# Packing the length-47 Fourier steps of a filter and mixer kernel into quarters of the TensorE array

## The chip, the cores and the metric

One core of one Trainium2 chip runs the whole kernel. The metric is the device time of one execution in microseconds. Three executions of the kernel before gave 2565.34, 2567.13 and 2570.79 us; the median, 2567.13 us, is the time before.

## The reference: what is computed

Two blocks follow each other, for a batch of 8 sequences of 3008 rows and 256 channels.

```python
def _attn_ref(x, filt_r, filt_i):            # x: (8, 3008, 256)
    X = np.fft.rfft(x, axis=1)
    F = (filt_r + 1j * filt_i)[None, :, :]   # filter: (1505, 256), real and imaginary part
    y = np.fft.irfft(X * F, n=x.shape[1], axis=1)
    return y.astype(np.float32)

def _moe_ref(x, w_tok1, w_tok2, w_ch1, w_ch2):   # (3008,256) (256,3008) (256,1536) (1536,256)
    xt = x.transpose(0, 2, 1)
    h = np.maximum(xt @ w_tok1, 0.0) @ w_tok2
    u = x + h.transpose(0, 2, 1)
    h2 = np.maximum(u @ w_ch1, 0.0) @ w_ch2
    return (u + h2).astype(np.float32)
```

The first block is a real Fourier transform along the sequence, a product with a complex filter, and the transform back. The second is an MLP mixer: a token MLP along the sequence, and a channel MLP on its sum with the input. All weights of the mixer arrive as 64-bit floats.

## The kernel before, in words

**The transform.** 3008 is 47 x 64. A row number is n2 * 47 + n1, with n2 below 64 and n1 below 47. The transform goes in three steps, forward and back:

- *Length 64* (`a_unit`, L471). One matmul takes two residues n1 = a (partitions 0 to 63) and n1 = a + 24 (partitions 64 to 127), with their 64 values of n2 on the partitions. The table `wa` gives, for each of 32 frequencies k2, four rows: real and imaginary part of either residue. Each matmul carries 2 values of a and 256 channels, so 512 columns. ScalarE copies the bank into `t1`, and a DMA from the ACT queue stores it in `z_d` in device memory, so that the next step can read it with the 96 rows (4 kinds x 24 values of a) of one k2 on the partitions.
- *Length 47* (`b_unit`, L537). For each k2 one matmul of 96 rows by 128 columns makes the real parts (columns 0 to 63) and imaginary parts (64 to 127) of the 47 frequencies that k2 stands for, for both batches of a group side by side (512 columns), or one batch (256).
- *The filter* (L550 to L553): four VectorE operations multiply the bank by the complex filter into `p1`.
- *Length 47 back* (`bi_unit`, L562): one matmul of 128 rows by 96 columns. ScalarE copies the bank into `t3` (L568), and after two frequencies a DMA from the ACT queue stores `t3` in `g_d` (L573).
- *Length 64 back* is no step of its own: `t4_load` (L619) reads `g_d` with the 128 rows of (k2, kind) on the partitions, and the mixer's matmuls take it from there (`token_sums` L625 with the table folded into `w1`, `u_filter` L647 with `wai`).

The batches form the groups (0), (1, 2), (3, 4), (5, 6), (7). Batch 0 keeps its z on the chip (`turned`), takes banks "pg", and multiplies real and imaginary filter at once (L545); its length-47 matmuls are a branch of their own.

**The mixer.** `mix` runs, for each batch and each of 6 row tiles m (512 rows, the last 448), 6 steps jp of 256 hidden channels: 36 items a batch. Its matrix products are done in blocks of two by two with seven products instead of eight, so VectorE adds blocks (helper `v`, L726) before and after them. An item issues, in this order:

1. `up_first` (L748, 4 products of 256 columns), `up_middle` (L726), then the block sums and the first part of `down` (L782, 3 products) of the item before; then place 0.
2. `up_last` (L764, 3 products, two L726 adds, each followed by a ReLU on ScalarE, L769); then place 1.
3. The second part of `down` (L782, 4 products), at a tile's end the first of the steps of `finish`; then place 2.

At certain items and places `u_parts` issues one of the four quarters (`u_quarter`, L669, L675) of the next tile's u, and after the last of them queues two VectorE steps (`v_steps`) and a weight load (`w2m_load`) on SP's queue.

**How the two are interleaved.** The order on every engine is the order in which the program is written (`tc.manual_schedule()`). The transform of the next group is a Python generator, `dft`; at a place that is "due" the loop at the end takes one step from it. For the groups after the first, one step is due at place 1 of each item: a length-64 step, or `b_unit(k)` followed by `bi_unit(k - 1)`. In the items of batch 0 the steps are spread over two places by a counter (L1006 to L1022).

**Banks.** Length-64 and length-47 matmuls, u-quarters and token sums use the two PSUM banks "acc" and "b" in turn:

```python
turn, held = ["acc", "b"], []

def free_bank():
    turn.reverse()
    if turn[0] in held:
        turn.reverse()
    return turn[0]
```

`b_unit` puts its bank into `held`, and `bi_unit` takes it out and writes the products back into the same bank.

**Loads.** `t2_load` (z, from SP's queue) and `w_load` (the length-47 tables `wb` from SP's queue and filter rows) are issued two chunks of two frequencies ahead, with `b_unit` of the even k.

Of the kernel before, what the change touches and what calls it, by code (L numbers as in the profile page):

```python
# [26 lines left out]
KR = 4 * A  # L27
HALF = 64
# [26 lines left out]
def _make_tables():  # L55

    n2 = np.arange(N2)
    wa = np.zeros((P, P))
    wai = np.zeros((P, P))
    for h in range(2):
        r = slice(h * 64, h * 64 + 64)
        for k2 in range(K2):
            th = 2 * np.pi * ((n2 * k2) % N2) / N2  # L70
            c, s = np.cos(th), np.sin(th)
            re, im = 4 * k2 + 2 * h, 4 * k2 + 2 * h + 1
            wa[r, re] = c
            wai[re, r] = c * (1.0 if k2 == 0 else 2.0)
            if k2 == 0:
                alt = 1.0 - 2.0 * (n2 % 2)
                wa[r, im] = alt
                wai[im, r] = alt
            else:
                wa[r, im] = -s  # L80
                wai[im, r] = -2.0 * s
    n1 = np.arange(N1)
    re = (n1 // A) * (2 * A) + n1 % A
    im = re + A
    wb = np.zeros((KR, K2, P))
    wi = np.zeros((P, K2, KR))
    for k2 in range(K2):
        for s in range(2 * A):
# [10 lines left out]
            if edge:  # L99
                sn = np.zeros(N1)  # L100
            if k2:
                wb[re, k2, q] = c
                wb[im, k2, q] = sign * sn
                wb[re, k2, HALF + q] = -sn
                wb[im, k2, HALF + q] = sign * c
            else:
                src = re if s < A else im
                wb[src, k2, q] = c
                wb[src, k2, HALF + q] = -sn
                m = 1.0 if edge else 2.0  # L110
                wi[q, k2, src] = m * c
                wi[HALF + q, k2, src] = -m * sn
    wi[:, 1:, :] = wb[:, 1:, :].transpose(2, 1, 0)
    wi /= N
    f = np.float32
    wbi = np.zeros((P, K2, P + KR))
    wbi[0:KR, :, 0:P] = wb
    wbi[:, :, P:] = wi

    wa0 = wa.reshape(P, K2, 4).transpose(0, 2, 1).reshape(P, P)  # L120
    wbi0 = wbi.copy()
    wbi0[:, :, 0:P] = 0
    wbi0.reshape(4, K2, K2, P + KR)[:, 0:A, :, 0:P] = wb.reshape(4, A, K2, P)
# [4 lines left out]
def kernel(  # L128
# [22 lines left out]

    z_d = nc.dram_tensor("z_tmp", (B, K2, KR, D), FP32, kind="Internal").ap()
    g_d = nc.dram_tensor("g_tmp", (B, K2, KR, D), FP32, kind="Internal").ap()
# [158 lines left out]
    def w1_load(i):  # L312
# [6 lines left out]
        for h in range(2):  # L319
            n = 1 if last and h else 2  # L320
            lo = h * A + 2 * i
            q.dma_start(st[h * HALF:(h + 1) * HALF, 0:n * DT].rearrange("p (a t) -> p a t", t=DT),
                        rows[:, lo:lo + n, :])
# [7 lines left out]
    def w2_load(i):  # L331
# [5 lines left out]
        more = g + 1 < W2G  # L337
        st = stage(512)
        nc.gpsimd.dma_start(st[:, 0:n + more], moe_w_tok2[ts(t, P), ds(g * NG * N1, n + more)])
# [3 lines left out]
        def some(h, nh, w):  # L343
            return (lambda v: bass.AP(tensor=v.tensor, offset=v.offset + h * A, ap=[v.ap[0], [A, nh], [N1, nn], [1, w]]),
                    dst[:, h:h + nh, :, 0:w])

        parts = [some(0, 2, A)] if more else [some(0, 1, A), some(1, 1, A - 1)]
        if i < BY_PE:
            h = halves(st, n + more, spare_pair())
            yield next(h)  # L350
            yield next(h)
            on_chip(ident, *next(h), n + more, parts)
        else:
            yield from rounded(st, n + more, parts, False)
# [90 lines left out]
    def x_load(b, c, i, queue=None):  # L445
# [9 lines left out]
        rows = x[b].rearrange("(n2 n1) d -> n2 n1 d", n1=N1)[:, :, ds(d0 * dc, dc)]  # L455
        for h in range(2):
            n = xc - 1 if h and (c + 1) * xc == A else xc
            lo = h * A + c * xc
            q = queue or (nc.gpsimd if b == 0 and h else nc.sync)
            q.dma_start(t[h * HALF:(h + 1) * HALF, 0:n, :], rows[:, lo:lo + n, :])  # L460
            if n < xc:

                q.dma_start(t[h * HALF:(h + 1) * HALF, n:xc, :], rows[:, lo:lo + 1, :])
        xs[b, c + d0 * (A // xc)] = t

    def rows_of(t_d, b):
        return t_d[b].rearrange("k (g a) d -> (k g) a d", a=A)
# [12 lines left out]
    def dft(bs):  # L480
# [5 lines left out]
        def table_load(c):  # L486
            if c * KC % WC == 0:
                g = c * KC // WC
                where, tag = (t1p, "t1") if first and g % 5 > 2 else (wbp, "wb")
                wbs[g] = where.tile([P, WC, P + KR], FP32, tag=tag, name="wb")  # L490
# [16 lines left out]
        if not first:  # L507
            yield True
        for i, u in enumerate(todo):
# [6 lines left out]
            yield i + 1 < len(todo)  # L516
# [7 lines left out]
        def t2_load(c):  # L524
            if first:
                return
            t2s[c] = t2p.tile([KR, KC, nb, D], FP32, tag="t2", name="t2")
            for i, b in enumerate(bs):
                nc.sync.dma_start(t2s[c][:, :, i, :], z_d[b, ts(c, KC)].rearrange("k r d -> r k d"))

        def b_unit(k):
            tag = "pg" if first else free_bank()
            if not first:
                held.append(tag)
            ps = bank(tag).rearrange("p (b d) -> p b d", b=2)[:, 0:nb, :]
            t2 = turned[:, k, :].unsqueeze(1) if first else t2s[k // KC][:, k % KC]
            nc.tensor.matmul(ps, wbs[k // WC][0:P if first else KR, k % WC, 0:P], t2, start=True, stop=True)  # L537
            re, im = slice(0, HALF), slice(HALF, P)
            t = filts_0[k // KC % len(filts_0)] if first else filts[k // KC % FB]
# [513 lines left out]
```

## Time and profile before

| What | Value |
|---|---|
| Median of three runs | 2567.13 us |
| Span of the profiled execution, first to last instruction | 2563.4 us |
| Median less span (start, end, and the spread of runs) | 3.7 us |
| TensorE matmul busy | 2485.5 us, 11204 instructions |
| VectorE busy | 1919.6 us |
| ScalarE busy | 680.1 us |
| GpSimd busy | 593.2 us |
| Mean granted TensorE clock | 0.994 |
| Moved by DMA | 248.37 MB in 166432 packets |

Busy time of an engine counts a stretch in which several of its instructions overlap once. "PEld" is TensorE's weight load, which runs beside the matmuls. A matmul's own duration includes the time until its last result is out, so the next one can start before it ends; the chain of waits shows how long each held the path. A group's line gives the mean duration of one, then the idle time of the engine just before such an instruction, and what ended that idle time. The page's tenths are busy shares of 40 equal slices of the span.

The length-64 matmuls of the groups lie at 144 to 226 us, 526 to 705 us, 1136 to 1315 us and 1746 to 1832 us of the span, and the length-47 matmuls at 240 to 462 us, 725 to 1023 us, 1335 to 1633 us and 1853 to 2124 us.

### The profile page before, as it was taken

To read this page: it belongs to the slowest core of one execution; us is meant where nothing else is said; L and a number is where in the kernel's file an instruction comes from. 1 tells how busy PE (TensorE), PEld (TensorE's weight loads), DVE (VectorE), ACT (ScalarE), POOL (GpSimd) and SP (SyncE) were. 2 spreads that over 40 slices of the span, in tenths; PEclk is the share of its full clock that TensorE was granted. 3 is DMA by queue.
4 is the path that set the end of the run, shared out by engine and by line. 5 is a ranking of instruction groups with operands and counts; after the bars stand their busy time and mean duration, and the time that the engine had idled before them with its cause. 6 is when DMAs were issued, how large, how long until landed. Compare 5 with 4: busy or idle time off the path is not lost.

```text
span 2563.4 us, 32297 instructions
## 1 busy us (share of the span) xinstructions
PE 2485.5 (97%) x11204; PEld 2049.0 (80%) x11204; DVE 1919.6 (75%) x3594; ACT 680.1 (27%) x1342; POOL 593.2 (23%) x1075
## 2 busy tenths in 40 slices
PE   7889999999999999999999999999999999999997
PEld 4557666888888777888888777898888888898887
DVE  7797888576686988756676899757788587757776
ACT  5633222122221222222222222212222122212222
POOL 6573222112111121121121111211211121211222
PEclk8999999999999999999999999999999999999999
DMA  9974344233332332213333333213333222101100
GB/s 220 248 218 134 118 125 146 70 115 109 116 108 72 107 96 83 81 57 125 101 101 93 97 106 102 85 32 111 103 109 97 58 76 71 44 29 36 43 14 20
DMA packets 166432, 248.37 MB, mean 97 GB/s; under 512 B 35300, under 2 KB 112474, under 8 KB 166270
## 3 DMA queue, kind: packets, MB, share of 16 engines
q1 hardware_dynamic: 93006, 150.24, 19.5%
q0 software_dynamic: 33312, 48.47, 7.5%
q10 hardware_dynamic: 39952, 47.61, 5.9%
q8 instruction: 89, 1.46, 0.2%
q14 instruction: 73, 0.60, 0.1%
HBM read 168.96 MB, written 77.22 MB: 96 GB/s over the span
## 4 chain that ended last, share of the span: by engine, by line
PE 74%; DVE 17%; DMA 4%; issue 2%; ACT 2%; POOL 1%; ACTq 0%; DVEq 0%; SPq 0%; POOLq 0%
PE ps_po L782 25%; PE ps_pg L748 15%; PE ps_pg L764 11%; PE ps_b L625 4%; DVE t L726 3%; DVE hh L726 3%; PE ps_acc L669 2%; PE ps_b L669 2%; PE ps_acc L625 2%; DVE u L726 2%; DVE s L726 2%; DMA filt<-in_filt_r_dram 2%; PE ps_acc L647 2%; PE ps_b L647 2%; PE ps_b L537 1%
## 5 line engine op out<-in xcount | busy, mean ns | idle before, releaser
L827 POOL DMA_DIRECT2D out_dram<-r x757 | 410.5, 551 | 1757.3 <-ACT hh L769 732.7
L726 DVE TENSOR_TENSOR hh<-ps_pg,s 128x512 f32<-128x512 f32 (+3 forms) x864 | 482.7, 586 | 342.2 <-ACT s L751 334.5
L769 ACT ACTIVATE hh<-hh 128x512 f32<-128x512 f32 (+1 forms) x576 | 348.0, 621 | 1200.4 <-DVE hh L726 1200.4
L782 PE MATMUL ps_po<-t,wc 128*128 128x256 f32 (+1 forms) x2304 | 535.7, 375 | 6.7 <-DVE t L726 5.7
L782 PEld LDWEIGHTS ps_po<-t,wc 128*128 128x128 f32 x2304 | 434.1, 190 | 131.8 <-issue 52.9
L748 PE MATMUL ps_pg<-v,wc 128*128 128x256 f32 (+1 forms) x1728 | 413.1, 375 | 3.1 <-DVE v L726 2.4
L782 PE MATMUL ps_po<-hh,wc 128*128 128x256 f32 (+1 forms) x1728 | 412.7, 375 | 0.9 <-POOL wc L363 0.7
L748 PEld LDWEIGHTS ps_pg<-v,wc 128*128 128x128 f32 x1728 | 327.4, 190 | 43.0 <-DVE v L726 5.1
L782 PEld LDWEIGHTS ps_po<-hh,wc 128*128 128x128 f32 x1728 | 327.9, 190 | 38.9 <-POOL wc L363 1.1
L764 PE MATMUL ps_pg<-u,wc 128*128 128x256 f32 (+1 forms) x1152 | 293.5, 377 | 7.2 <-DVE hh L726 7.1
L726 DVE TENSOR_TENSOR t<-t,hh 128x256 f32<-128x256 f32 (+1 forms) x576 | 245.8, 427 | 19.8
L764 PEld LDWEIGHTS ps_pg<-u,wc 128*128 128x128 f32 x1152 | 216.1, 190 | 43.5 <-DVE hh L726 18.4
L726 DVE TENSOR_TENSOR s<-ps_pg,hh 128x512 f32<-128x512 f32 (+1 forms) x288 | 196.0, 681 | 30.4 <-DVE hh L726 0.5
L726 DVE TENSOR_TENSOR t<-hh 128x512 f32<-128x512 f32 (+1 forms) x288 | 193.0, 670 | 0.6 <-ACT hh L769 0.6
L751 ACT COPY s<-ps_pg 128x256 f32<-128x256 f32 (+1 forms) x288 | 105.9, 368 | 312.3 <-PE ps_pg L748 308.5
L748 PE MATMUL ps_pg<-u,wc 128*128 128x256 f32 (+1 forms) x576 | 169.1, 375 | 3.9 <-DVE hh L726 3.9
L764 PE MATMUL ps_pg<-v,wc 128*128 128x256 f32 (+1 forms) x576 | 168.7, 375 | 0.0
L748 PEld LDWEIGHTS ps_pg<-u,wc 128*128 128x128 f32 x576 | 109.0, 190 | 28.9 <-issue 11.0
L764 PEld LDWEIGHTS ps_pg<-v,wc 128*128 128x128 f32 x576 | 108.7, 190 | 13.1
L726 DVE TENSOR_TENSOR u<-ps_acc,u 128x512 f32<-128x512 f32 (+3 forms) x105 | 61.1, 582 | 76.5 <-PE ps_acc L669 60.0
L625 PE MATMUL ps_b<-t,w 128*128 128x256 f32 x480 | 104.6, 379 | 1.1 <-ACT t L568 1.1
L726 DVE TENSOR_TENSOR u<-ps_b,u 128x256 f32<-128x256 f32 (+3 forms) x105 | 59.5, 566 | 61.3 <-PE ps_b L669 42.3
(133 smaller groups left out, 2528.6 us busy)
## 6 DMA issues: line engine op xcount, KB each, us to landing
w<-w_tmp SPq DMA_DIRECT2D x35, 896.0 KB
g_tmp<-t ACTq DMA_DIRECT2D x128, 192.0 KB
out_dram<-r POOLq DMA_DIRECT2D x698, 32.0 KB, 1.8
z_tmp<-t ACTq DMA_DIRECT2D x84, 256.0 KB
t<-z_tmp SPq DMA_DIRECT2D x112, 192.0 KB
t<-g_tmp SPq DMA_DIRECT2D x42, 512.0 KB
wb<-wbi_t SPq DMA_DIRECT2D x80, 224.0 KB
x<-in_x_dram SPq DMA_DIRECT2D x139, 128.0 KB
```

Of the source, the lines that this page charges most:

```text
L537: nc.tensor.matmul(ps, wbs[k // WC][0:P if first else KR, k % WC, 0:P], t2, start=True, stop=True)
L625: nc.tensor.matmul(acc[:, t, :], w1[:, a, ts(t, P)], t4[b, a // TC4][:, a % TC4, :], start=(a == 0 and t == 0), stop=(a == A - 1 and t == ...
L647: nc.tensor.matmul(ps[:, ds(q * P, n)], t4[b, c][:, r, ts(dh, P)], wai[:, 0:n], start=(first and q == 0), stop=(not first and q == 3))
L669: nc.tensor.matmul(ps[:, ds(j * hw, hw)], h1[:, n, :], w2m[m % 2][:, at, 0:hw], start=(i < 2 and j == 0), stop=(j == len(todo) - 1))
L726: nc.vector.tensor_tensor(out=out, in0=in0, in1=in1, op=op)
L748: nc.tensor.matmul(ps[:, 0:hw], chan[0][:, jp, n, :], mov, start=True, stop=True)
L751: nc.scalar.copy(out=s[:, 0], in_=g[0][:, 0, 0:hw])
L764: nc.tensor.matmul(ps[:, 0:hw], chan[0][:, jp, n, :], mov, start=True, stop=True)
L769: nc.scalar.activation(out=hs, in_=hs, func=AF.Relu)
L782: nc.tensor.matmul(po[i][:, j, 0:hw], chan[1][:, jp, n, :], mov, start=(jp == 0 and first == 1), stop=(jp == JP - 1 and last == 1))
L827: q.dma_start(rows[g, e, :, ds(h * A + 4 * m, n)], blocks[ts(g, CW), h, e, 0:n])
```

## The change: what it does

The rows of the input are taken in mirrored pairs. A length-64 matmul now takes residue 23 - a in partitions 0 to 63 and residue 24 + a (shifted by one in n2 where it wraps around) in partitions 64 to 127, so that the two stand at equal distances from the middle. Its table gives, instead of real and imaginary parts of either residue, sums and differences of the pair. With these the length-47 step falls into two independent blocks: 48 of the 96 rows make the real outputs and the other 48 make the imaginary outputs. A block is 48 rows by 64 columns, and backward 64 rows by 64 columns, of which 48 are used.

Two frequencies are then taken together. For odd k2 the two blocks' places are swapped, so that the four blocks of an even and an odd frequency lie in the four 64 x 64 quarters of the array: frequency i and row half h write output half h XOR i of bank i. `b_pair` makes the two frequencies of a chunk in both banks, `multiply` does the four VectorE operations of one frequency, and `bi_pair` goes back, two banks again. A chunk is now three steps of the generator: `b_pair` with the first `multiply` and the loads for two chunks ahead; the second `multiply`; and `bi_pair` with its two ScalarE copies and two stores. For the groups after the first, one chunk takes two items: `b_pair` at place 1 of an odd item, the second `multiply` at place 0 of the next even one, `bi_pair` at place 0 of the next odd one. The u-quarters move to places at which a bank is free.

`z_d` and `g_d` become one tensor for each group, with the group's batches side by side, so that loads of z and stores of g move one 2 KB run for two batches. Because the residues of one half run backward, the loads of x and of `w_tok1`, the rounding of `w_tok2` and the stores of the output go through that half with a negative step. Batch 0 keeps its branch of full matmuls with new tables.

The core of the diff:

```diff
         for h in range(2):
             n = xc - 1 if h and (c + 1) * xc == A else xc
-            lo = h * A + c * xc
             q = queue or (nc.gpsimd if b == 0 and h else nc.sync)
-            q.dma_start(t[h * HALF:(h + 1) * HALF, 0:n, :], rows[:, lo:lo + n, :])
+            q.dma_start(t[h * HALF:(h + 1) * HALF, 0:n, :],
+                        rows(A + c * xc if h else A - 1 - c * xc, [[N1 * D, N2], [D if h else -D, n]]))
...
+        def four(pss, stat, mov):
+            for i, ps in enumerate(pss):
+                for h in range(2):
+                    to = slice((h ^ i) * HALF, (h ^ i) * HALF + HALF)
+                    nc.tensor.matmul(ps[to], stat(i, h), mov(i, h), start=True, stop=True)
+
+        def b_pair(c):
+            prods[c] = two_banks()
+            held.extend(turn)
+            four(prods[c], lambda i, h: wbs[c][ds(h * HALF, KH), i, 0:HALF], lambda i, h: t2s[c][ds(h * HALF, KH), i])
+
+        def multiply(c, i):
+            ps, t = prods[c][i], filts[c % FB]
             re, im = slice(0, HALF), slice(HALF, P)
...
             nc.vector.tensor_tensor(out=p1, in0=ps, in1=fr, op=ALU.mult)
             nc.vector.scalar_tensor_tensor(out=p2[re], in0=ps[im], scalar=-1.0, in1=fi, op0=ALU.mult, op1=ALU.mult)
             nc.vector.tensor_tensor(out=p2[im], in0=ps[re], in1=fi, op=ALU.mult)
             nc.vector.tensor_tensor(out=p1, in0=p1, in1=p2, op=ALU.add)
+            prods[c][i] = p1
+            held.pop(0)
+
+        def bi_pair(c):
+            pss, p = two_banks(), prods.pop(c)
+            four(pss, lambda i, h: wbs[c][ts(h, HALF), i, HALF:P], lambda i, h: p[i][ts(h, HALF)])
+            t3 = t3p.tile([P, KC, nb, D], FP32, tag="t3", name="t3")
+            for i in range(KC):
+                by_block(t3[:, i], pss[i])
+            for h in range(2):
+                nc.scalar.dma_start(g_d[place_of[bs[0]][0]][ts(c, KC), ts(h, KH)].rearrange("k r b d -> r k b d"),
+                                    t3[ds(h * HALF, KH)])
...
+        if not first:
+            for c in range(K2 // KC):
+                b_pair(c)
+                multiply(c, 0)
+                if c + 2 < K2 // KC:
+                    t2_load(c + 2)
+                    w_load(c + 2)
+                yield "m"
+                multiply(c, 1)
+                yield "i"
+                bi_pair(c)
+                if c + 1 < K2 // KC:
+                    yield "b"
+            return
...
-        own = ({(3, 2): 0, (4, 2): 1}, {(2, 2): 0, (3, 0): 1, (3, 2): 2, (4, 0): 3})
-        new = {(JP - 3, 2): 0, (JP - 2, 0): 1, (JP - 2, 2): 2, (JP - 1, 0): 3}
+        own = ({(3, 2): (0,), (4, 2): (1,)}, {(2, 2): (0,), (4, 0): (1,), (4, 2): (2, 3)})
+        new = {(JP - 2, 0): (0,), (JP - 2, 2): (1, 2, 3)}
...
-            due = place == 1
             if group == 0:
-                due = spread
-                if not spread and place:
-                    at += 1
-                    due = at * left // places > (at - 1) * left // places or at > places
+                due = coming in "aw" or place > 0 or (coming == "m" and i % 4 == 2)
+            elif coming in "bmi":
+                due = i % 2 == (coming != "m") and place == (coming == "b")
+            else:
+                due = place == 1
```

`coming` is the kind of the step that is next: a length-64 step ("a"), the wait for the loads ("w"), `b_pair` ("b"), the second `multiply` ("m") or `bi_pair` ("i").

## The prediction

> **What bounds the kernel now.** I read the page first, then the windows view cut by stages, then the chain of waits inside one stage that the change touches, and last the groups with shapes kept apart.
>
> The page:
>
> ```profile
> span 2563.4 us, 32297 instructions
> PE 2485.5 (97%) x11204; PEld 2049.0 (80%) x11204; DVE 1919.6 (75%) x3594; ACT 680.1 (27%) x1342; POOL 593.2 (23%) x1075
> PE   7889999999999999999999999999999999999997
> DMA  9974344233332332213333333213333222101100
> ```
>
> TensorE is busy from the third slice to the end; the DMA engines are full only in the first two slices. The windows view says how much room the other engines have, first where the length-64 matmuls of batches 3 and 4 run (544 to 683), then where their length-47 matmuls run (856 to 1008). Columns are window, length, then the busy time of PE, PEld, DVE, ACT and POOL, the clock, DMA share and GB/s.
>
> ```profile
> 544.30:683.00 138.70, 138.70 (x632) 115.95 (x631) 94.58 (x180) 39.58 (x78) 25.58 (x48) 1.00 0.35 110
> 856.00:1008.00 152.00, 151.09 (x639) 115.95 (x638) 139.27 (x248) 40.16 (x77) 26.00 (x48) 1.00 0.34 98
> ```
>
> In the second window PE has 0.9 us idle of 152, but VectorE has only 12.7 us idle (92% busy; 68% in the first). TensorE is the bound and VectorE stands close behind, just where the change saves or adds matmul time. The chain of waits in that stage, with start, length, engine, tile, line and number of instructions:
>
> ```profile
> 1004.28 1.10 PE ps_b L537 x2
> 1005.38 0.86 PE ps_acc L562 x2
> 1006.24 1.73 PE ps_po L782 x8
> 1007.97 0.89 PE ps_acc L647 x8
> ```
>
> An fp32 product appears as two instructions ("passes"). Eight passes of 256 columns hold the path for 1.73 us, so 0.216 us each; two of 512 columns hold it 0.86 us, 0.43 us a pass. Each pass starts when the one before has streamed. (1.10 includes a restart after a wait.) The groups by form:
>
> ```profile
> L537 PE MATMUL ps_b<-t,wb 96*128 96x512 f32 x96 | 50.2, 604 | 3.7 <-ACT u L658 2.6 <-ACT t L568 0.5 <-DVE u L726 0.2
> L537 PE MATMUL ps_acc<-t,wb 96*128 96x512 f32 x96 | 49.8, 599 | 1.9 <-ACT u L658 1.4 <-DVE u L726 0.2
> L562 PE MATMUL ps_acc<-p,wb 128*96 128x512 f32 x96 | 49.4, 595 | 3.6 <-DVE p L553 3.6
> L562 PE MATMUL ps_b<-p,wb 128*96 128x512 f32 x96 | 49.3, 594 | 2.9 <-DVE p L553 2.9
> L562 PEld LDWEIGHTS ps_acc<-p,wb 128*96 128x96 f32 x160 | 26.0, 165 | 33.1 <-issue 21.8 <-DVE p L553 7.0 <-ACT t L568 1.5
> L553 DVE TENSOR_TENSOR p<-p,p 128x512 f32<-128x512 f32 x96 | 66.5, 693 | 3.3
> ```
>
> A pass lasts 594 to 604 ns but the next starts 430 ns after it: a tail of 0.17 us is normally covered by the next pass. The weight load of 165 ns is covered too. There are 192 passes of 512 columns on L537, so 96 products forward (three groups of two batches, 32 frequencies each), and 96 back on L562.
>
> **What goes.** For three groups 192 products at 0.86 us: 165 us. For the last batch alone 64 products of 256 columns at 0.43 us: 27.5 us. Together 192.6 us of path, 7.5% of the span. Batch 0 has its own branch and keeps its products.
>
> **What comes on TensorE.** Two frequencies are now four products forward and four back, each 48 or 64 rows by 64 columns, with the full 512 (or 256) moving columns. That is eight passes where there were four. The calls come product after product, so the two passes of one product (same tile) stand next to each other: t0 t0 t1 t1 t2 t2 t3 t3. If different tiles may overlap but starts stay in program order, as every start in this trace does, t0's second pass waits 0.43 us for its first; t1's first starts with it; t1's second waits again, and so on: five steps of 0.43 us instead of four. There are 128 such sets (16 pairs, two directions, four groups): 96 at 512 columns, 32 at 256. 96 x 5 x 0.43 + 32 x 5 x 0.216 = 241 us against 192.6: **+48 us**. The bounds: all four tiles together take two steps, 96 us in all, which is -96; no overlap at all takes eight steps, which is +193. No row here has a tiled matmul. I take five because program order is what the rows show.
>
> The Trainium skill, "TensorE: Matmul & The Clock Gate", The mechanism, says matmuls start and end strictly in order, and that tiles of a pack start about 4 ns apart. No tile runs in this trace; its span model, for one instruction per tile, would make a set of single passes about 0.6 us and speaks for the two-step bound, while its order rule with two passes per product gives the five steps.
>
> **Changing shape.** A set always stands between full-array matmuls (after L782 or L764, before L764 or L782), so there are 256 changes between the whole array and quarters. If the tail of 0.17 us must run out at each: 256 x 0.17 = **+43 us**. Bounds: nothing (the trace goes from 96*128 to 128*96 to 128*128 with no gap on the chain) and 0.17 plus an uncovered weight load of 0.19 (190 ns in the L782 rows): +92. No gain is possible, since an exposed tail only adds. I take 0.17, nearest to a plain end-to-start order. The skill's page "TensorEngine Tiling (Array Packing)", Key Properties, says a change of tiling mode drains the array; that speaks against this change and would make the sum +43 where the L537 to L562 rows alone would make it nothing.
>
> **VectorE and the order of steps.** The four products with the filter per frequency stay: 0.68 + 0.69 + 0.68 + 0.69 = 2.75 us. They came once an item, after the two L726 adds that free the pg banks. Now the first set comes in an odd item's place 1 and the second in the next even item's place 0, ahead of those adds. The adds (0.69 us each) hold up the next L748. Over two items VectorE has 15.1 us busy (139.27 in 18.4 items of 8.25 us) of 16.5; if PE grows by 1.54 us per pair (twice 0.43 for the fifth steps, four tails of 0.17), VectorE's 1.4 us of room doubles and the delay hides. Cover gone, it is up to 1.3 us (the two adds) on 48 pairs: 62 us. I take 0; it is the cover that fails in the rival below. The forward set waits for both banks, so for two ACT copies (0.57 us each on L568) after the backward set of the same item; the six L764 passes between (1.29 us) cover all but about 0.1 us. Behind it on PE would stand L782, on VectorE the multiply. The mixer's four u-quarters move from four places to (2,2), (4,0) and (4,2); their 4.7 us per tile of PE work is the same, and the v sums that follow still have item 5 ahead of the next tile. At nothing.
>
> **DMA and the rest.** x halves and z stores go from 2 KB to 1 KB runs, t4 loads from 4 KB to 1 KB, while z loads and g stores go from 1 KB to 2 KB and tables from 224 to 128 KB: some 23,000 pieces more (x 5,400, z stores 6,900, t4 10,400, from the tiles' partitions and counts) against 18,400 fewer, a net near 5,000 of 166,432 packets, and 6 MB fewer of 248 (64 tables, 96 KB each). At a DMA share of 0.34 these stay hidden; loads of z and tables are issued a pair ahead, some 30 us. If not covered, a late z load shows as a PE wait on L537; the chain in this stage had two pieces of 2.18 us on that load. In the first 180 us, where DMA is the bound, only w_tok1's runs halve (768 pieces; 0.195 x 16 x 2563 us / 93006 = 86 ns a packet, over 16 engines 4 us): 0 to +4, taken as 0, since the page has filter loads and not these ones at the head of the chain. w_tok2's rounding writes two halves in place of one: 14 tiles beside those loads, at nothing; SP, POOL and ACT issue as many DMAs as before, but one more per step for the last batch.
>
> **Sum.** +48 + 43 = +91 us on the profiled 2563.4: 2654.5. The median of the runs, 2567.13, lies 3.7 us above that span, which I take for what lies around it: **2658 us**. Own range: tails at nothing to 0.36 us give +48 to +140, so 2615 to 2707.
>
> **Rivals.**
> *All four tiles at once.* If the second pass of a product does not hold back the next tile, a set takes 0.86 us: -96 + 43 = -53 us, 2514. For it: the four products lie in four different quarters of the array, and write disjoint halves of two banks. Against: the start order seen, and VectorE: in the 152 us window there are only 12.7 us to gain, and the second multiply now stands ahead of the adds. If a quarter of the gain goes there: -40, **2527** (2505 to 2555). It decides as soon as a set stays under 1.38 us: four old steps (1.72) less two tails (0.34).
> *The two row halves run as separate streams.* Then three steps a set: -48 + 43 = -5: **2562**.
> *The tiles do not overlap*, so the change does not do what it says: eight steps: +193 + 43 = +236, **2803**. For it: no overlap of streams is in the trace; against: nothing in the code makes the tiles depend on each other.
>
> **Chances.** Five steps 0.46, four at once 0.38, row halves 0.08, serial 0.08. The measurement can tell about 0.2%, 5 us. Faster: nearly all of the second (0.36) and half of the third (0.04): 0.40. Same: 0.05. Slower: 0.55. The range 2515 to 2705 leaves out the serial case and the tips of the two main ones. The likeliest alone: 2615 to 2707.
>
> **What would show it.** In the profile after, passes of 48*64 and 64*64 come eight to a set. Right: within a set starts alternate between pairs a few ns apart and gaps of 0.43 us, a set takes 2.15 us, and before and after it PE idles about 0.17 us. Wrong: starts of all tiles together, a set near 0.9 us, VectorE above 92% in this stage and PE waiting on L726; or no shared starts and sets of 3.4 us. The stage's item grows from 8.25 us to about 9.0 us in my case (half of 1.54 more), and the 544 to 683 stage, which has no tiles, stays at its pace. A PE wait on L537 for a load would be a cost I put at nothing.

## The result, and the profile after

The changed kernel takes 2613.11 us (median of 4 runs, 2607.77 to 2615.97) against 2567.32 us for the kernel before: ratio 1.0177, 95% interval 1.0163 to 1.0192. It is slower by 46 us. The profiled span grew by 49.0 us, from 2563.4 to 2612.4. The page after:

```profile
span 2612.4 us, 33382 instructions
PE 2469.4 (95%) x11716; PEld 1982.0 (76%) x11716; DVE 1919.3 (73%) x3600; ACT 675.4 (26%) x1348; POOL 594.7 (23%) x1077
PE   7889887899999999999999999999999999999997
PEclk8999899999999999999999999999999999999999
```

TensorE is busy 16 us less and yet the span is longer. What is new is one place in the tenths, from the fifth to the eighth slice (261 to 522 us), where TensorE falls from 9 to 8 and 7 tenths; in the fifth the granted clock falls from 9 to 8 tenths.

The first token-sum matmuls of the eight batches cut the span into stages. The differences after less before, in us, are: to batch 0's token sums 0.0; batch 0 +46.7; then +0.4, +0.1, +1.3, +0.5, +0.3, -1.1 and +0.8. So the loss lies in batch 0's items, beside which the transform of batches 1 and 2 runs, and nothing is won elsewhere. The windows view shows both halves of this, first of the kernel before and then of the one after. Columns: window, length, busy time of PE, PEld, DVE, ACT, POOL, then the granted clock, DMA share and GB/s.

```profile
235.00:455.00 220.00, 207.41 (x818) 147.02 (x817) 183.21 (x315) 56.22 (x106) 67.00 (x112) 1.00 0.44 131
880.00:980.00 100.00, 99.39 (x423) 76.45 (x423) 90.10 (x159) 25.59 (x49) 17.33 (x32) 1.00 0.35 98
```

```profile
235.00:455.00 220.00, 179.95 (x761) 112.23 (x762) 151.65 (x262) 44.12 (x84) 49.19 (x84) 0.92 0.38 100
880.00:980.00 100.00, 93.85 (x466) 70.16 (x465) 89.14 (x158) 23.89 (x48) 17.46 (x32) 1.00 0.36 97
```

In the steady stage (second lines) TensorE's busy time falls by 5.5 us in 100, VectorE's stays, and the pace is the same: TensorE waits where it worked. In batch 0's stage every engine does less in the same 220 us, and the mean granted clock is 0.92: no engine is full (TensorE 82% busy), so a chain of waits sets the pace.

A set in the steady stage, from the timeline of TensorE (start, length, line, tile, number of passes):

```profile
909.79 1.03 PE L813 MATMUL ps_po<-hh,wc 128*128 128x256 f32 x4
910.75 0.65 PE L565 MATMUL ps_acc<-p,wb 64*64 64x512 f32 x2
910.76 0.65 PE L565 MATMUL ps_b<-p,wb 64*64 64x512 f32 x2
911.23 0.59 PE L565 MATMUL ps_acc<-p,wb 64*64 64x512 f32 x2
911.24 0.60 PE L565 MATMUL ps_b<-p,wb 64*64 64x512 f32 x2
911.77 1.13 PE L795 MATMUL ps_pg<-u,wc 128*128 128x256 f32 x4
```

The rows with ps_acc and ps_b hold two quarters each. All four first passes start within some 20 ns, all four second passes 0.48 us later, and the next full matmul 0.54 us after that: two steps, not five. The four L813 passes have streamed at 909.79 + 4 x 0.216 = 910.65, so the set starts 0.10 us later; its second step takes 0.11 us more than a pass of 0.43; its first step 0.05; and the four L795 passes take 0.10 us more than the usual 1.03. That is 0.36 us more than two bare steps would cost, which is put down here to going in and out of quarters, and 1.2 us for a set that cost 1.72.

What TensorE waited for between 235 and 502 us (total us, times, longest):

```profile
PE ps_b L565 <- DVE p L582: 13.3, 5, 2.9
PE ps_pg L795 <- DVE hh L757: 11.4, 5, 3.0
PE ps_acc L565 <- DVE p L582: 8.2, 3, 3.1
```

L582 is the last of the four filter operations: the backward set waits for the second multiply of its pair, 21.5 us in all. In the kernel before, the same wait in the same stage (117 to 474.5 us, token sums to token sums) was 6.5 us:

```profile
PE ps_acc L562 <- DVE p L553: 3.6, 4, 1.3
PE ps_b L562 <- DVE p L553: 2.9, 3, 1.1
```

With the waits goes a slower clock. Over its stage of 404.1 us the changed kernel has TensorE busy for 342.4 us at a mean granted clock of 0.95; the kernel that goes one frequency at a time beside batch 0 (below) has it busy for 324.8 of 358.9 us at 1.00, with as many matmuls. Of the 45.2 us between them, 17.6 us are then longer busy time, which fits the clock (404 x 0.05 = 20), and 27.6 us are idle time. This is an estimate from the two windows.

### The profile page after: what moved, and what is told of

Same layout as the page of the kernel before. It is cut to its first block, busy times and chain, and to the rows that moved or that the text cites. A ratio compares the mean times of both kernels' runs of the same rounds, so it can differ in the third digit from the quotient of the medians.

```text
span 2612.4 us, 33382 instructions
## 1 busy us (share of the span) xinstructions
PE 2469.4 (95%) x11716; PEld 1982.0 (76%) x11716; DVE 1919.3 (73%) x3600; ACT 675.4 (26%) x1348; POOL 594.7 (23%) x1077
## 4 chain that ended last, share of the span: by engine, by line
PE 64%; DVE 20%; issue 2%; ACT 2%; DMA 1%; DVEq 0%; ACTq 0%; POOL 0%; SPq 0%; POOLq 0%
PE ps_po L813 22%; PE ps_pg L779 14%; PE ps_pg L795 9%; PE ps_acc L656 6%; DVE t L757 4%; DVE hh L757 3%; PE ps_b L700 3%; DVE p L581 2%; DVE p L580 2%; DVE s L757 2%; DVE u L757 2%; DVE p L579 2%; PE ps_acc L700 2%; PE ps_b L565 2%; PE ps_acc L678 2%
## 5 line engine op out<-in xcount | busy, mean ns | idle before, releaser
L757 DVE TENSOR_TENSOR hh<-ps_pg,s 128x512 f32<-128x512 f32 (+3 forms) x864 | 482.8, 587 | 362.1 <-ACT s L782 347.5
L813 PE MATMUL ps_po<-t,wc 128*128 128x256 f32 (+1 forms) x2304 | 550.4, 382 | 10.0 <-DVE t L757 8.6
L813 PEld LDWEIGHTS ps_po<-t,wc 128*128 128x128 f32 x2304 | 432.0, 192 | 149.5 <-issue 33.9
L779 PE MATMUL ps_pg<-v,wc 128*128 128x256 f32 (+1 forms) x1728 | 416.5, 377 | 0.2
L813 PE MATMUL ps_po<-hh,wc 128*128 128x256 f32 (+1 forms) x1728 | 414.1, 376 | 0.2 <-ACT hh L800 0.2
L779 PEld LDWEIGHTS ps_pg<-v,wc 128*128 128x128 f32 x1728 | 329.1, 191 | 41.4 <-DVE v L757 3.0
L813 PEld LDWEIGHTS ps_po<-hh,wc 128*128 128x128 f32 x1728 | 329.0, 191 | 39.0 <-ACT s L782 0.7
L795 PE MATMUL ps_pg<-u,wc 128*128 128x256 f32 (+1 forms) x1152 | 297.4, 381 | 18.5 <-DVE hh L757 18.0
L795 PEld LDWEIGHTS ps_pg<-u,wc 128*128 128x128 f32 x1152 | 212.9, 190 | 83.6 <-DVE hh L757 34.9
L757 DVE TENSOR_TENSOR t<-t,hh 128x256 f32<-128x256 f32 (+1 forms) x576 | 245.3, 426 | 19.8
L757 DVE TENSOR_TENSOR s<-ps_pg,hh 128x512 f32<-128x512 f32 (+1 forms) x288 | 196.1, 681 | 32.6 <-DVE hh L757 1.8
L779 PE MATMUL ps_pg<-u,wc 128*128 128x256 f32 (+1 forms) x576 | 174.8, 385 | 23.9 <-DVE hh L757 23.8
L757 DVE TENSOR_TENSOR t<-hh 128x512 f32<-128x512 f32 (+1 forms) x288 | 192.7, 669 | 0.6 <-ACT hh L800 0.6
L795 PE MATMUL ps_pg<-v,wc 128*128 128x256 f32 (+1 forms) x576 | 169.4, 376 | 0.0
L779 PEld LDWEIGHTS ps_pg<-u,wc 128*128 128x128 f32 x576 | 105.9, 190 | 62.3 <-DVE hh L757 36.8
L656 PE MATMUL ps_acc<-t,w 128*128 128x256 f32 x672 | 146.5, 379 | 2.5 <-DVE p L581 2.5
L656 PEld LDWEIGHTS ps_acc<-t,w 128*128 128x128 f32 x672 | 127.4, 190 | 20.5 <-DVE p L581 3.5
L757 DVE TENSOR_TENSOR u<-ps_b,u 128x256 f32<-128x256 f32 (+3 forms) x124 | 69.7, 562 | 86.2 <-PE ps_b L700 60.0
L795 PEld LDWEIGHTS ps_pg<-v,wc 128*128 128x128 f32 x576 | 108.9, 190 | 13.4 <-DVE s L757 0.6
```

Source lines behind the costliest of these rows:

```text
L656: nc.tensor.matmul(acc[:, t, :], w1[:, a, ts(t, P)], t4[b, a // TC4][:, a % TC4, :], start=(a == 0 and t == 0), stop=(a == A - 1 and t == ...
L757: nc.vector.tensor_tensor(out=out, in0=in0, in1=in1, op=op)
L779: nc.tensor.matmul(ps[:, 0:hw], chan[0][:, jp, n, :], mov, start=True, stop=True)
L795: nc.tensor.matmul(ps[:, 0:hw], chan[0][:, jp, n, :], mov, start=True, stop=True)
L813: nc.tensor.matmul(po[i][:, j, 0:hw], chan[1][:, jp, n, :], mov, start=(jp == 0 and first == 1), stop=(jp == JP - 1 and last == 1))
```

## The experiments

The measure besides the total is the pace of one row tile beside length-47 sets: the difference between the starts of the first L779 (before: L748) matmul of row tiles 1 and 2 of batch 2. It is 52.39 us before and 52.95 us after. "Batch 0's stage" is the time from batch 0's first token-sum matmul to batch 1's: 357.4 us before, 404.1 after. Its length moves by some us without any change to it: the kernel of "The second multiply later" issues the same steps in this stage and took 397.3 us there, 6.8 less than the changed kernel. Differences of that size in this stage tell nothing.

### Two quarters in place of four

Does the overlap of four quarters matter? Here both frequencies of a pair use the same two quarters.

```diff
-                    to = slice((h ^ i) * HALF, (h ^ i) * HALF + HALF)
+                    to = slice(h * HALF, h * HALF + HALF)
```
and the tables without the swap for odd k2.

> Both frequencies of a pair use the same two quarters of the array, tables to match: four steps a set in place of two, all else as in the changed kernel. If TensorE bounded the stages of batches 1 to 7, each of 128 sets costs its two steps more: 96 x 0.86 + 32 x 0.43 = +96 us, 2709. If VectorE bounds them now, TensorE's idle time there takes up part: about 2 us more per row tile in place of 5.2, +30 to +60 in all, 2645 to 2675.

Measured: 2668.91 us (1.0392, 1.0362 to 1.0422), row tile 57.05 us, batch 0's stage 405.6. The total is as the second theory had it, the row tile is not: it rose by twice the 2 us named. So the four quarters save 4.1 us a row tile of the six sets' 5.16, and in batch 0's stage nothing that stands out. With TensorE's steps as many as before, this kernel takes 57.05 - 52.39 = 4.7 us a row tile more than the kernel before. Some 2.2 us of that are changes of shape, if each of six sets pays the 0.36 us seen above; the rest is the new order of steps. The quarters win nearly all of it back.

### In what order the quarters start

```diff
-            for i, ps in enumerate(pss):
-                for h in range(2):
+            for h in range(2):
+                for i, ps in enumerate(pss):
```
on top of the two-quarter kernel.

> Two quarters used twice, as in the kernel with two tiles, but the products are issued quarter by quarter: both frequencies' products of the first quarter, then both of the second. If matmuls start strictly in program order, the second quarter's first pass waits until the first quarter's fourth has started: seven steps of 0.43 us a set in place of four, 3.0 us, and 2740 or more. If each quarter works off its own row of passes, a set stays at four steps, 1.7 us, and the total within 6 us of 2669.

Measured: 2699.29 us (1.052, 1.0489 to 1.0550), batch 0's stage 437.1, but the row tile 57.08 us, as with the other order. The total missed what was expected of either theory; the pace of the steady stages, where the set itself is seen, did not. The timeline of TensorE:

```profile
931.78 1.08 PE L563 MATMUL ps_acc<-p,wb 64*64 64x512 f32 x4
932.69 1.03 PE L563 MATMUL ps_b<-p,wb 64*64 64x512 f32 x4
933.65 1.13 PE L793 MATMUL ps_pg<-u,wc 128*128 128x256 f32 x4
```

Bank acc's products are the first and the third in the program, one for each quarter; b's are the second and the fourth. The four passes of acc run first, then the four of b, 1.87 us from the first to the next full matmul. So the third product started before the second: a quarter does not wait for another quarter's earlier products, once these can run.

In batch 0's stage, 31 us longer than with the other order, the timeline shows another side of this:

```profile
319.48 1.07 PE L563 MATMUL ps_b<-p,wb 64*64 64x512 f32 x2
323.64 1.11 PE L563 MATMUL ps_acc<-p,wb 64*64 64x512 f32 x1 [3.09 <-DVE p L580]
323.65 1.11 PE L563 MATMUL ps_b<-p,wb 64*64 64x512 f32 x1
```

Here bank b's products are the first and the third. The third needs no more than the first, but it started only when the second, which waits for the second multiply (L580), could start too. So a product that waits for a semaphore did hold up those behind it. With the other order both products of the first bank come ahead of that wait. TensorE was busy for 380.5 us of this stage at a mean granted clock of 0.93, against 354.1 us at 0.97 with the other order; that is 26 of the 31 us.

### VectorE made light, in both kernels

Three of the four filter operations are left out, so that the output holds the product with the real part of the filter alone. What is left shows the time without that VectorE work.

```diff
-            nc.vector.scalar_tensor_tensor(out=p2[re], in0=ps[im], scalar=-1.0, in1=fi, op0=ALU.mult, op1=ALU.mult)
-            nc.vector.tensor_tensor(out=p2[im], in0=ps[re], in1=fi, op=ALU.mult)
-            nc.vector.tensor_tensor(out=p1, in0=p1, in1=p2, op=ALU.add)
```

Before, with this edit:

> The kernel before with one of the four filter operations left (real part of the filter alone), so VectorE has 2.07 us less for each frequency. Theory: TensorE bounds the stages of batches 1 to 7, a row tile beside length-47 products falls from 52.4 to no less than 51.2 (its matmul time), 2540 to 2562 in all with what batch 0's items gain. Rival (VectorE's order bounds before too): 48 or less.

After, with this edit:

> The changed kernel with one of the four filter operations left. Theory (four quarters save 0.5 us a set on TensorE, and VectorE's operations take its place): the row tile beside length-47 sets falls from 52.95 to 48 to 49.5 us, 2 to 4 us under the kernel before with the same operations left out; batch 0's loop gets 4.1 us shorter a pair and its stage falls by 20 to 50 us; 2515 to 2570 in all. Rival (changes of shape or copies through ScalarE eat the gain): 51 us or more.

Measured: before 2537.04 us (0.9887, 0.9859 to 0.9916) with 51.70 us a row tile; after 2496.48 us (0.9729, 0.9701 to 0.9758) with 48.37 us, both lower in all than expected. Windows of the two, before first:

```profile
880.00:980.00 100.00, 99.84 (x430) 78.00 (x429) 67.86 (x127) 26.53 (x51) 14.05 (x27) 1.00 0.33 96
```

```profile
880.00:980.00 100.00, 100.00 (x510) 77.12 (x509) 73.76 (x138) 27.17 (x53) 17.32 (x32) 1.00 0.33 86
```

TensorE is full in both, and the quarters are worth 51.70 - 48.37 = 3.33 us a row tile, 0.55 us a set. With the filter's full work all of that is lost and 0.56 us besides: VectorE's work in the new order costs 4.6 us a row tile (52.95 - 48.37), in the old 0.7. Batch 0's stage is 344.7 us before and 343.9 after: with 4.1 us less of VectorE's work in a pair's loop the 46.7 us are gone too.

### The filter's sum on GpSimd

```diff
-            nc.vector.tensor_tensor(out=p1, in0=p1, in1=p2, op=ALU.add)
+            nc.gpsimd.tensor_tensor(out=p1, in0=p1, in1=p2, op=ALU.add)
```

After, with this edit:

> The last of the four filter operations (the sum, 0.69 us) goes from VectorE to GpSimd, in all groups but batch 0's. Theory (VectorE's load takes the place of the matmul time saved): a row tile beside length-47 sets falls from 52.95 us by 2 to 4 us, batch 0's stage by 5 to 20: 2565 to 2595 in all. Rival (the order of the steps and the chains through ScalarE set the time, or GpSimd's slower sum delays the backward set): within 8 us of 2613, or above it.

Before, with this edit:

> The kernel before with the sum of the filter on GpSimd. Theory: before, TensorE bounds the stages of batches 1 to 7 (99% busy), so taking 0.69 us per frequency from VectorE changes a row tile by less than 0.3 us there and the total by less than 8 us, apart from batch 0's items. Rival (VectorE bounded before too): 15 to 30 us faster.

Measured: after 2618.31 us (1.0195, 1.0166 to 1.0225), as the rival had it; the row tile fell by 1.5 us to 51.5, less than the theory said, and batch 0's stage grew by 18 to 422.1. Before: 2632.81 us (1.0257, 1.0231 to 1.0282), slower, which neither theory had. The stages of batches 2 and 4, beside length-47 products, grew by 11 and 16 us, those of batches 5 and 6 by 5 and 8, and batch 0's grew by 31 to 388.3. The sum takes 1.27 us there (0.69 on VectorE), and PE waited for it on L562 for 38.5 us in 12 waits up to 1000 us, up to 9.7 us at once. Before the longest of these waits ended, GpSimd did this:

```profile
369.50 7.61 POOL L827 DMA_DIRECT2D out_dram<-r  x14 [3.34 <-ACT t L568]
377.85 1.09 POOL L827 DMA_DIRECT2D out_dram<-r  x2 [0.74 <-DMA out_dram<-r]
378.95 1.27 POOL L553 TENSOR_TENSOR p<-p,p 128x512 f32<-128x512 f32 x1
```

The sum stood behind sixteen stores of the output. A queue that also issues these is no place for a step that a matmul waits for so soon. In the changed kernel's steady stages the row tile did fall, so there the lighter VectorE outweighs the slower sum.

### The second multiply later

```diff
-                due = i % 2 == (coming != "m") and place == (coming == "b")
+                due = i % 2 == (coming != "m") and place == (coming != "i")
```

> For the groups after the second the second multiply moves from place 0 to place 1 of the even item, behind the two sums that free the pg banks; the load on each engine is the same. If the order on VectorE eats the gain, a row tile beside length-47 sets falls from 52.95 by 1 to 3 us: 2590 to 2607 in all. If it is the load, within 4 us of 2613.

Measured: 2658.67 us (1.0352, 1.0322 to 1.0382), row tiles of 54 to 57 us. Neither was expected. The order on VectorE does matter, but place 1 is worse than place 0: PE waited on L581 (the last reader of the bank) before the u-quarters L700 and L678 for 19.6 us between 770 and 1090 us, where the changed kernel waited 5.5 us for it. So the bank is held longer here. How much of the loss this makes, and what the two sums gained by going first, the run doesn't separate.

### Batch 0's items: another pace for the pairs

```diff
-                due = coming in "aw" or place > 0 or (coming == "m" and i % 4 == 2)
+                due = coming in "aw"
+                if not due:
+                    at += 1
+                    due = at % 9 in (0, 3, 4, 7)
...
+                if group == 0 and coming == "m":
+                    coming = next(todo, "end")
```

> In the items of batch 0 both multiplies of a pair come in one step and the backward set comes three places (one item) later, in place of one or two; nothing else changes. Theory A (the 46.7 us that batch 0's stage grew are the wait of the backward set for its second multiply, with the slower clock that follows such a wait): the stage falls from 404 us towards the 357 us of before, by 25 to 45 us, to 2570 to 2590 in all, with the granted clock of that stage back near 1.00 from 0.94. Rival B (both banks held, or VectorE's load beside the conversions): within 10 us of the changed kernel, 2605 to 2620. In both the later stages stay as they are.

Measured: 2620.56 us (1.0204, 1.0174 to 1.0234), batch 0's stage 410.7 us. The wait for L582 is gone, and others took its place (117 to 527 us):

```profile
PE ps_pg L779 <- DVE hh L757: 33.8, 11, 4.7
PE ps_acc L686 <- DVE p L581: 12.6, 4, 3.4
PE ps_po L813 <- DVE u L757: 11.1, 4, 2.9
```

Two multiplies in a row, 5.5 us, stand ahead of the sums that free the pg banks, and hold both banks that `u_unit` (L686) needs. At this pace the wait moved and the time stayed; theory A in the form stated (the short distance alone) fell.

### One frequency at a time, with the quarters kept

Here everything of the change stays (mirrored residues, tables, layouts, quarters), but a step is again one frequency in one bank, two quarters forward, and the backward set of the frequency before it in the other bank.

```diff
+            for k in range(K2 + 1):
+                if k < K2:
+                    b_one(k)        # two quarters, bank free_bank(), then multiply
...
+                if k >= 1:
+                    bi_one(k - 1)   # two quarters, the other bank
+                yield "s"
```

For all groups, with the places of the u-quarters of before and its counter beside batch 0:

> All tables, layouts and quarters of the change stay, but a step makes one frequency in one bank (two quarters at a time), and the order of steps, places of the u-quarters and the two banks in turn are those of before: two frequencies are in flight, one in each bank. Theory A (a pair that holds both banks leaves one serial loop of forward set, two multiplies, backward set and copies, and in batch 0's items VectorE's other work lengthens that loop): batch 0's stage goes back to 357 to 367 us from 404. A set of one frequency takes 0.86 us like a full product plus about 0.25 for two changes of shape, so a row tile beside length-47 sets costs 2 to 3 us more than before, 54.5 to 55.5: 2585 to 2605 in all. Rival B (the quarters, the new layouts or tables cost batch 0's items their time): that stage stays above 390 us and the total above 2620.

For the group beside batch 0 alone, with that counter:

> Only the group of batches 1 and 2, which runs beside batch 0, goes one frequency at a time with before's counter; the later groups keep the pairs of the change. Theory A: batch 0's stage 357 to 367 us, all later stages as in the changed kernel: 2567 to 2580. Rival B: 2610 or more.

The same, with the later groups' sum on GpSimd:

> As the kernel with one frequency at a time beside batch 0, and in the later groups the sum of the filter on GpSimd. The row tiles beside length-47 sets fell by 1.5 us with that sum on GpSimd while its slower 1.27 us per sum cost batch 0's items; here batch 0's items don't have it. Theory A: 2552 to 2567, 10 to 15 us under the kernel without it. Rival (GpSimd's other work suffers): no difference or more.

Measured: for all groups 2556.97 us (0.9960, 0.9944 to 0.9976), batch 0's stage 357.8, row tile 51.25. For the group beside batch 0 alone: 2570.93 us (1.0013, 1.0004 to 1.0022), stage 358.9, row tile 53.28. With the sum on GpSimd: 2555.89 us (0.9957, 0.9941 to 0.9974), stage 357.2, row tile 51.48. All of batch 0's loss goes with the pair and its pace, so the layouts, tables and changes of shape cost that stage nothing that can be seen. And the first of these kernels is 0.4% faster than the kernel before, and so is the last; the expected cost of 2 to 3 us a row tile did not come, because forward and backward set are issued one after the other and lie in different quarters:

```profile
931.95 0.65 PE L581 MATMUL ps_b<-t,wb 48*64 48x512 f32 x2
931.96 0.65 PE L591 MATMUL ps_acc<-p,wb 64*64 64x512 f32 x2
932.43 0.60 PE L581 MATMUL ps_b<-t,wb 48*64 48x512 f32 x2
932.44 0.59 PE L591 MATMUL ps_acc<-p,wb 64*64 64x512 f32 x2
```

They share the two steps, as four quarters of one direction do in the change. This keeps the overlap on TensorE and the old rhythm on VectorE. In its steady window (880 to 980 us) VectorE is busy 92.03 of 100 us and TensorE 96.52, against 90.10 and 99.39 in the kernel before.

### One bank, no burst

Beside batch 0 the kernel goes one frequency at a time in one bank. A counter spreads the steps so that nearly every place takes one: a forward set with its multiply, then, one place later, its backward set.

```diff
-            tag = free_bank()
+            tag = "acc"
...
+            for k in range(K2):
+                b_one(k)
...
+                yield "s"
+                bi_one(k)
+                yield "s"
```

> Beside batch 0 one frequency at a time, as in the hybrid kernel, but always in bank acc: the forward set of the next frequency comes one place after the backward set of this one, so one loop is in flight and there is no burst of two multiplies. Later groups as in the changed kernel. Theory A (one serial loop in flight costs batch 0's stage its time): the stage grows from 357 to 380 us or more, 2593 or more in all. Rival (the burst of two multiplies on VectorE, which delays the mixer's sums): the stage stays at 357 to 367, 2568 to 2580.

Measured: 2622.28 us (1.0220, 1.0190 to 1.0249), batch 0's stage 411.2 us. PE waited 35.1 us in 19 waits for the multiply before L591. There is no burst here, only one bank is held, and one frequency is in flight; the loss is as large as with the pair. One thing differs besides: a frequency alone has no other set to share its steps with, so that 64 sets cost some 1.2 us each where the changed kernel has 32. TensorE is busy for 361.3 us of this stage, some 37 us more than with two frequencies in flight, and part of the loss may be that. (Two quarters in place of four also gave TensorE 27 us more of steps in this stage, and there its length hardly changed.)

Taken together the runs say this of batch 0's stage. It is the pair that costs it its time: with one frequency in each of two banks, and all else of the change kept but the pace of the steps, 45 of the 46.7 us are gone. What the pair brings is that one unit of work must go forward set, multiply, backward set, copies before the next may start: the wait for the multiply is seen in the changed kernel and with one bank, and with a shorter multiply (and VectorE lighter by as much) the loss is gone. At the three paces tried (the changed kernel's, a burst at a long distance, one bank) the wait fell on the backward set or on the mixer's sums, and the stage stayed at 397 to 411 us. That no pace of the pairs could do better is not shown.

## Why the prediction was right, and where its steps failed

**The sign and the range held, for other reasons than those given, and that is luck.** The time of 2613.11 lies within 2515 to 2705, slower as the likeliest case had it, but 45 us below its 2658 and just under its own range of 2615 to 2707. The term that was to make it slower made it faster, and two terms that were put at nothing, or not put at all, made it slower.

**Five steps a set: wrong.** The step "starts stay in program order, as every start in this trace does" took a row of full-array matmuls for a rule of quarters. A set takes two steps, so the term of +48 us was -96. The Trainium skill's order rule ("TensorE: Matmul & The Clock Gate", The mechanism: matmuls start and end strictly in order) does not hold for these quarters: in the order experiment the third product started with the first. Its 4 ns between the tiles' starts is near what is seen: four starts within some 20 ns here.

**Changes of shape: right in size.** +43 us was said, 0.34 us a set; the set shown above has 0.36. They do not lie where they were put, as a tail of 0.17 us at each change: 0.10 us stand ahead of the set, 0.16 within it and 0.10 in the matmuls behind it. Quarters and changes together were -53 us in the rival of four tiles at once, 0.52 us a 512-column set; the light kernels show 0.55.

**VectorE at nothing: wrong.** The text saw the second multiply ahead of the sums and priced it at 0 to 62 us, but took 0 because it let PE grow. With PE shrinking the cover was gone, as the rival said. The rival gave a quarter of the 53 us to it; in the stages after batch 0's, where some 34 us of the saving lie, all of it went. That is 3.33 + 0.56 = 3.9 us a row tile of three pairs, 1.3 us a pair, which is just the price that the text gave to the uncovered delay. That it is the delay of the two sums is not shown: with the second multiply behind them the time rose. What the runs do show is that VectorE's work in this order takes it (light kernels), and that the old order with the same work does not (one frequency at a time, 51.25 us). The rival's clause "in the 152 us window there are only 12.7 us to gain" was the better reading of the same line.

**Batch 0's stage: not in the sum at all.** For the group beside batch 0, the diff's first branch of the pace takes a step at places 1 and 2 of every item, and at place 0 of some. So a pair does not have the two items there that the groups after it have; 16 pairs ran in some 22 items. The kernel before did this stage's 32 frequencies from 240 to 462 us, 13.9 us for two, where two items of the later stages are 16.5 us. The loop of a pair is a forward set (about 1.2 us with the changes), two multiplies (5.5), a backward set (1.2) and copies (1.2), 9 us of chain in that time, before anything else on those engines gets in between. One pair in flight could not keep the old pace, and the stage grew by 46.7 us, nearly the whole result.

In the terms of the sum, as an estimate from the rows above: -96 for two steps a set; +46 for the changes (128 sets at 0.36); +36 for VectorE in the later stages (their 2.2 us of growth and the 34 us of saving that they lost); +63 for batch 0's stage (46.7 us of growth and 16 of saving lost). Together that is +49, against 49.0 measured. The last two terms are what was left over in their stages, so the sum closes by itself; what it shows is the size of each.

**Kept:** the stage without quarters stayed at its pace (46.22 us a row tile in both kernels). The change moved 6.2 MB fewer, as said, but in 10,907 packets more, not near 5,000; no cost of it shows, and the longest wait of TensorE for a load in batch 0's stage is 1.3 us.

Of the predicted sights, "a set near 0.9 us" (1.02 from its first pass to the next full matmul) and "PE waiting on L726" (now L757) came true for the rival; "VectorE above 92%" did not: it stayed at 89, since VectorE waits in its turn. An engine need not look full to be the bound when its order is the bound.

**Open:** how much of the 46.7 us is one loop in place of two, and how much is the second bank that a pair holds besides. The waits in the changed kernel speak for the loop (21.5 us for the multiply, 6.6 us of `u_unit` for the bank's last reader), but no run separates the two cleanly.

## What to carry to other kernels

When a change makes work on the bounding engine shorter by grouping two units, count the units in flight per buffer before counting the saving: the pair took both banks, and with one loop in place of two the change lost more than four quarters of the array saved. Look at each stage in which the grouped work runs, above all at the one where it must come fastest: here 13.9 us for two frequencies, not 16.5. Small matmuls of different steps can share the array as well as those of one step, so put into the quarters what is due at the same time anyway.

## What the runs showed of the hardware that was not expected

- Quarters of 64 x 64 overlap in fp32, both passes of a product included (four starts within some 20 ns, four more 0.48 us later), and also between matmuls of different shape (48 and 64 rows, 931.95 us). They start out of program order when they can run (931.78 us), but one that waits for a semaphore held up those behind it (319.48 us). Two products in the same quarters follow each other: four steps took 1.87 us.
- TensorE's granted clock fell to half around long waits, for a few us at a time. In the changed kernel TensorE waited 3.08 us for the second multiply of a pair, until 314.46 us. The chain of waits has this of the passes that came next, and the windows view has the clock, 0.50 and then 1.00 (columns as above):

```profile
314.46 1.97 PE ps_acc L565 x4
316.43 3.71 PE ps_po L813 x8
```

```profile
314.50:320.20 5.70, 5.70 (x16) 2.90 (x20) 1.72 (x3) 2.19 (x4) 3.38 (x7) 0.50 0.35 75
320.40:324.00 3.60, 3.60 (x21) 2.51 (x14) 2.62 (x4) 0.37 (x1) 3.60 (x8) 1.00 0.67 169
```

  Eight passes of 256 columns took 3.71 us of path, where the same took 1.73 us in the kernel before. So after this wait of 3 us they took some 2 us more. In the kernel before, where no wait of TensorE in this stage was over 1.7 us, the mean clock of the stage is 1.00. How long a wait must be is not shown.
- Two row halves wrote to different partitions of one bank in the same step (bank acc's two products at 910.75 us, which start together).
